# DeltaNet followed by hash routing on one core: 64-column products, another order of the products, and another start and end of the first phase

## The chip, the cores and the metric

One core of a Trainium2 chip. The metric is device microseconds (us) of one execution of the whole kernel; all data are float32. Engines are named as in the profile: PE is TensorE, PEld its weight loads, DVE VectorE, ACT ScalarE, POOL GpSimd, SP the queue from which most DMAs are issued.

## The reference

```python
# q, k, v: (4, 8, 768, 48), beta: (4, 8, 768); token_ids: 3072; w1: (8, 384, 1024); w2: (8, 1024, 384)
k_n = k / (norm(k) + 1e-6)
state = 0                                   # (4, 8, 48, 48)
for t in range(768):
    y[t] = q[t] @ state
    v_old = state.T @ k_n[t]
    state += beta[t] * outer(k_n[t], v[t] - v_old)
x = y as (3072, 384)                        # token = batch and position, columns = head and element
expert = token_ids * 2654435761 % 8
out[token] = relu(x[token] @ w1[expert]) @ w2[expert]
```

## The kernel before, in words

Phase 1 computes `y`. The 768 steps are cut into `NU` = 24 chunks of `C` = 32 steps. Inside a chunk the recurrence becomes a triangular system, so that a chunk is a handful of matrix products; only the 48x48 states go from chunk to chunk. The 32 pairs of batch and head are packed four to a tile of 128 partitions (four blocks of 32), which gives `NT` = 8 tiles, in two halves `h` of `HT` = 4. The state of two heads lies in 96 partitions.

The products of one half of one chunk, each with what comes after it:

- `ks`: old state times K into `psK`. It is written as two products of 64 columns for each tile (`pair(p)`); VectorE then makes `R = V - psK` (L487).
- `ys`: state times Q into `psY`, one product of 128 columns for each tile with 96 moving columns (L494).
- `w`: the inverted triangular matrix `TB` times `R` into `psW`, 128 columns, 48 moving (L500); ScalarE copies it to `W` in two instructions (L504).
- `s`: `K4` times `W`, added to the state in `psS` (L510); ScalarE copies it to `S` (L516).
- `ym`: the masked Gram matrix `MB` times `W`, added to `psY`, 128 columns, 96 moving (L520); of the 96 columns that result, half are used in either half of the partitions. ScalarE copies `psY` to `x_sb` in two instructions (L527), and `store_x` sends it to memory.

Every float32 product appears in the profile as two matmul instructions.

A set is what four chunks of one batch need: `turn_heads` transposes K and Q of a set on TensorE (L347) and spreads them (`sd`, `KT`, `QT`) with ScalarE and, for the first four sets, VectorE; `gram` multiplies them (L382); `gram_out` copies the products to `NT` (ScalarE) and, masked, to `MT` (VectorE, L394). Four sets make a group, enough for four chunks. `invert(g)` inverts a group's triangular matrices on VectorE alone: a chain of some 80 dependent instructions with 31 steps of two tensor_tensor each (L436, L438), at its end the transposition `TU` (L441). It is a generator with an estimate in us ahead of each piece, and `inv.do(us)` issues pieces up to that sum. `spread` copies a chunk's part of `MT` and `TU` into the block-diagonal tiles `MB` and `TB` by four DMAs each, from the SP queue.

The order is written out by hand in one loop over `c` from -9 to 23: every engine runs its instructions in the order of that loop. Iteration `c` computes chunk `c`, turns set `c+9`, multiplies set `c+8`, inverts a quarter of group `c//4+1`, and loads two chunks ahead (`load_k4` and `load_v` from the POOL queue, `load_kq` from SP). From the iteration after 16 on, `routing` (one-hot ranks of the tokens, mostly VectorE, with three groups of matmuls) is advanced two to four pieces at the end of each iteration; its two products `rp` (L221, L222) and the four groups `gp` (L317) wait for VectorE. Weights of the first expert are loaded at the end of iteration 16.

Before the loop, 16 DMAs of `beta` are issued from ScalarE's queue (L160), POOL builds constants and clears 11 tiles (L180), and VectorE makes the mask `low` (L175).

Phase 2 gathers the tokens of each expert and runs the two products (L636, L650). The change does not touch it.

The loop of one iteration before:

```python
ks(c, 0); inv.do(2.4); ys(c, 0); w(c, 0); ks(c, 1); s(c, 0); s_out(c, 0); ym(c, 0); y_out(c, 0); w(c, 1)
inv.do(5.6); scale_v(c + 1); store_x(c - 1); turn_k(ut); tq = turn_q(ut)
ys(c, 1); s(c, 1); s_out(c, 1); next(tq); gram(ug, 0); ym(c, 1); y_out(c, 1)
gram(ug, 1); gram_out(ug); spread(MT, MB); spread(TU, TB)
```

Of the kernel before, what the change touches and what calls it, by code (L numbers as in the profile page):

```python
# [18 lines left out]
def kernel(  # L19
# [12 lines left out]
    P = 128  # L32
# [52 lines left out]
    with ExitStack() as phase1:  # L85
# [22 lines left out]
        def quarter(q):  # L108
            return slice(C * q, C * q + C)
# [42 lines left out]
        load_kq(0)  # L152
        load_kq(1)

        beta_i = st.tile([P, NG, C], F32)
        beta_r = beta.rearrange("b (g q) (n c i) -> q c (b g) n i", q=4, c=GC, i=C)
        for i in range(4):
            for j in range(GC):
                p0 = C * i + NT * j
                nc.scalar.dma_start(out=beta_i[p0:p0 + NT], in_=beta_r[i, j])  # L160
# [18 lines left out]
        for t in W2s + TBs + MBs + K4s:  # L179
            nc.gpsimd.memset(t, 0.0)  # L180


        def routing():
# [34 lines left out]
            yield  # L218
# [3 lines left out]
            nc.tensor.matmul(rp[:, 1], lhsT=ones, rhs=oh, start=True, stop=True)  # L222
            rank = rt.tile([P, E, NTC], F32)
# [4 lines left out]
            yield  # L228
# [5 lines left out]
            yield  # L234
# [14 lines left out]
            yield  # L249
# [9 lines left out]
            yield  # L259
# [14 lines left out]
                                    op=ALU.mult)  # L274
            yield
            col = rt.tile([P, E, NTC], F32)
            for i in range(1, KT + 1):
# [11 lines left out]
            yield  # L289
# [16 lines left out]
                                    op=ALU.mult)  # L306
            yield
            val = rt.tile([P, NHI], F32)
            G = 6
            for g in range(NTC // G):  # L310
                lo = rt.tile([P, G, P], F32, name="lo")
                nc.vector.tensor_tensor(
                    lo, iota_f[:, None, :].to_broadcast([P, G, P]),
                    part[:, 1, g * G:(g + 1) * G, None].to_broadcast([P, G, P]), op=ALU.is_equal)
                gp = ps_t.tile([P, NHI], F32, tag="t")
                for i in range(G):
                    nc.tensor.matmul(gp, lhsT=lo[:, i], rhs=hi[:, g * G + i],  # L317
                                     start=(i == 0), stop=(i == G - 1))
                if g == 0:
                    nc.vector.tensor_copy(val, gp)  # L320
                else:
                    nc.vector.tensor_tensor(val, gp, val, op=ALU.add)
                yield
# [14 lines left out]
            yield  # L338
# [4 lines left out]
        def turn_heads(u, x, dst, a):  # L343
            g, b = divmod(u, B)
            psT = ps_t.tile([D2, H // 2, GC, C], F32, tag="t", name="psT")
            for i in range(H // 2):
                nc.tensor.transpose(psT[:, i].rearrange("p j s -> p (j s)"),  # L347
                                    x[:, 2 * i:2 * i + 2].rearrange("p h d -> p (h d)"), ident)

            sd = sds[u][:, :, a].rearrange("p j i s -> p i j s")  # L350
# [5 lines left out]
            yield  # L356
# [7 lines left out]
        def turn_k(u):  # L364
            sds[u] = pre.tile([D2, GC, 2, H // 2, C], F32, tag="sd", bufs=2, name="sd")
            for _ in turn_heads(u, Kd.pop(u), KTs, 0):
                pass

        def turn_q(u):
            return turn_heads(u, Qd.pop(u), QTs, 1)  # L370
# [15 lines left out]
        def gram_out(u):  # L386
# [3 lines left out]
            psG = psGs.pop(u)  # L390
            del sds[u]
            nc.scalar.activation(NTs[g][:, :, :, 2 * b:2 * b + 2].rearrange("p t j g -> p g j t"),
                                 psG[:, :, :, 0], ACT.Copy)
# [66 lines left out]
        def spread(src, dst):  # L460

            for i in range(4):
                nc.sync.dma_start(out=dst[quarter(i), :, i, :], in_=src[quarter(i)])
# [25 lines left out]
        def ys(c, h):  # L489
            Ys[h] = ps_y.tile([P, HT, 2, D], F32, tag="y", name="psY")  # L490
            if c == 0:
                return
            for i, QT in enumerate(tiles(QTs, c, h)):
                nc.tensor.matmul(Ys[h][:, i], lhsT=QT.rearrange("p u x -> p (u x)"),  # L494
                                 rhs=Ss[h][:, i], start=(i == 0), stop=True, skip_group_check=True)

        def w(c, h):
            psW = ps_w.tile([P, HT, D], F32, tag="w", name="psW")
            for i in range(HT):
                nc.tensor.matmul(psW[:, i], lhsT=TBs[c % 2][:, HT * h + i], rhs=Rs[h][:, i],  # L500
                                 start=True, stop=True, skip_group_check=True)
# [16 lines left out]
        def ym(c, h):  # L518
            for i in range(HT):
                nc.tensor.matmul(Ys[h][:, i], lhsT=MBs[c % 2][:, HT * h + i], rhs=Ws[h][:, i],  # L520
                                 start=(c == 0 and i == 0), stop=True, skip_group_check=True)

        def y_out(c, h):
            if h == 0:
                xs[c] = wk.tile([P, NT, D], F32, tag="x_sb", bufs=2, name="x_sb")
            for p in range(2):
                nc.scalar.activation(xs[c][pair(p), HT * h:HT * h + HT], Ys[h][pair(p), :, p],  # L527
                                     ACT.Copy)
# [8 lines left out]
        route = None  # L537
        inv = Work(iter(()))
        for c in range(-9, NU):
            step = c >= 0  # L540
            ut, ug = c + 9, c + 8
            turns, grams = ut < NU, 0 <= ug < NU
            if c % GC == 0 and c // GC + 1 < NG and c >= -GC:
                inv = Work(invert(c // GC + 1))
            if ut + 2 < NU:
                load_kq(ut + 2)
            if c >= -4 and c + 2 < NU and c + 2 >= 0:
                load_k4(c + 2)
                load_v(c + 2)
            if step:  # L550
                ks(c, 0)
            inv.do(2.4 if step else 3.0)
            if step:
                ys(c, 0)
                w(c, 0)
                ks(c, 1)
                s(c, 0)
# [5 lines left out]
            if c + 1 >= 0 and c + 1 < NU:  # L563
                scale_v(c + 1)
            if c >= 1:
                store_x(c - 1)
            if turns:
                turn_k(ut)
                tq = turn_q(ut)
            else:  # L570
                tq = iter(())
            if step:
                ys(c, 1)
                s(c, 1)
                s_out(c, 1)
            next(tq, None)
            if grams:
                gram(ug, 0)
# [3 lines left out]
            for _ in tq:  # L582
                pass
            if grams:
                gram(ug, 1)
                gram_out(ug)
            if -1 <= c < NU - 1:
                n = c + 1
                spread(MTs[n // GC % 3][:, n % GC], MBs[n % 2])
                spread(TUs[n // GC][:, n % GC], TBs[n % 2])  # L590
            if route is not None:
# [172 lines left out]
```

## Time and profile before

| what | us |
|---|---|
| time, median of 3 runs (lowest to highest) | 746.71 (745.66 to 749.37) |
| the profiled execution, its own time | 746.85 |
| its span | 745.2 |
| PE busy (share of the span) | 645.9 (87%) |
| DVE busy | 286.6 (38%) |
| ACT busy | 206.0 (28%) |
| POOL busy | 190.7 (26%) |
| chunk 0 begins (first `w`) | 65.17 |
| chunk 15 begins | 281.95 |
| phase 1's last `ym` begins | 406.10 |
| phase 2's first gemm begins | 426.64 |

The profile is of one execution. Its page gives busy shares of each engine over the whole span; since phase 1 and phase 2 have different limits, the same shares are asked for by stretches, and then the instructions of one chunk in order of time. The rows merge neighbouring instructions of one kind and one line into one row with a count, and a square bracket says how long the engine sat idle just before and who released it. PEclk is the clock that TensorE was granted, as a share of 2.4 GHz: 0.5 is 1.2 GHz.

### The profile page before, as it was taken

What the parts mean: (1) busy time and instruction counts of PE and PEld (TensorE: products, weight loads), DVE (VectorE), ACT (ScalarE), POOL (GpSimd) and SP (SyncE); (2) the same over time, 40 slices, a digit from 0 to 9 for tenths busy, and PEclk for the clock granted to TensorE, in tenths of its full rate; (3) what the DMA queues carried; (4) which work ended last, traced back from release to release, by engine and by line L of the source; (5) the groups of instructions that cost most, each with busy time, mean ns of one, the idle gap of its engine ahead of it and who ended that gap; (6) DMA issues with size and microseconds to landing.
All of it is one profiled execution on the core that took longest, in us unless ns stands there. A gap on an engine that the chain in (4) does not pass through costs nothing. (4 is left out here: it accounts for less than half of the span.)

```text
span 745.2 us, 11251 instructions
## 1 busy us (share of the span) xinstructions
PE 645.9 (87%) x4212; PEld 474.3 (64%) x4212; DVE 286.6 (38%) x725; ACT 206.0 (28%) x461; POOL 190.7 (26%) x293
## 2 busy tenths in 40 slices
PE   4545989998998999958988399999999999999995
PEld 3435888888888888857878155555555555555552
DVE  7697564574762584756421211111212110212110
ACT  2633454564545454312302010101011111101010
POOL 9200432243233225323400601040404040202022
PEclk9955787798878689868957599999999999999998
DMA  7622444354444333832410893242424220101011
GB/s 143 129 39 48 94 86 85 70 106 93 85 89 83 58 57 72 224 62 53 88 26 18 263 352 112 84 145 84 149 84 152 84 65 0 31 0 32 0 35 30
DMA packets 151112, 65.39 MB, mean 88 GB/s; under 512 B 134089, under 2 KB 143155, under 8 KB 151057
## 3 DMA queue, kind: packets, MB, share of 16 engines
q1 hardware_dynamic: 139920, 45.66, 25.5%
q0 software_dynamic: 10240, 18.89, 10.3%
q8 instruction: 35, 0.57, 0.3%
q10 hardware_dynamic: 896, 0.10, 0.1%
q14 instruction: 21, 0.16, 0.1%
HBM read 49.67 MB, written 10.22 MB: 80 GB/s over the span
## 5 line engine op out<-in xcount | busy, mean ns | idle before, releaser
L636 PE MATMUL h_ps<-xT,w_sb 128*128 128x448 f32 x384 | 147.4, 544 | 0.0
L650 PE MATMUL y_ps<-h_sb,w_sb 128*128 128x448 f32 x384 | 146.1, 539 | 0.0
L636 PEld LDWEIGHTS h_ps<-xT,w_sb 128*128 128x128 f32 x384 | 73.7, 192 | 72.1 <-issue 71.9
L650 PEld LDWEIGHTS y_ps<-h_sb,w_sb 128*128 128x128 f32 x384 | 72.2, 190 | 67.6 <-issue 67.6
L144 POOL DMA_DIRECT2D K<-in_k_dram x96 | 55.6, 586 | 194.8 <-PE psS L510 193.5
L641 DVE TENSOR_SCALAR h_sb<-h_ps 128x448 f32<-128x448 f32 x32 | 20.0, 625 | 168.3 <-PE h_ps L636 168.3
L619 POOL DMA_INDIRECT xg<-x_scratch,gx x32 | 31.9, 997 | 189.0 <-PE xT_ps L628 138.0
L500 PE MATMUL psW<-R,TB 128*128 128x48 f32 x368 | 58.8, 312 | 20.0 <-DVE R L487 20.0
L500 PEld LDWEIGHTS psW<-R,TB 128*128 128x128 f32 x368 | 56.3, 233 | 23.0 <-DVE R L487 22.8
L520 PE MATMUL psY<-W,MB 128*128 128x96 f32 x384 | 70.4, 344 | 0.2 <-ACT W L504 0.2
L520 PEld LDWEIGHTS psY<-W,MB 128*128 128x128 f32 x384 | 65.3, 256 | 1.5 <-ACT W L504 0.3
L438 DVE TENSOR_TENSOR U<-U,tmp 128x31 f32<-128x31 f32 (+15 forms) x186 | 63.7, 342 | 6.4
L436 DVE TENSOR_TENSOR tmp<-U,Ni 128x31 f32<-128x31 f32 (+15 forms) x186 | 63.5, 342 | 5.6
L510 PE MATMUL psS<-W,K 128*96 128x96 f32 x368 | 56.5, 317 | 6.9 <-ACT W L504 5.5
L664 POOL DMA_INDIRECT out_dram<-o_sb,gidx x32 | 30.5, 953 | 120.9 <-ACT o_sb L662 111.0
L494 PE MATMUL psY<-S,QT 96*128 96x96 f32 x368 | 59.1, 312 | 0.8 <-ACT x_sb L527 0.8
L510 PEld LDWEIGHTS psS<-W,K 128*96 128x96 f32 x368 | 49.5, 222 | 9.9 <-ACT W L504 7.7
L150 POOL DMA_DIRECT2D V<-in_v_dram x96 | 55.3, 583 | 1.8 <-issue 1.7
L494 PEld LDWEIGHTS psY<-S,QT 96*128 96x128 f32 x368 | 53.1, 222 | 2.9 <-ACT x_sb L527 1.4
L504 ACT ACTIVATE W<-psW 64x192 f32<-64x192 f32 x96 | 31.1, 324 | 81.5 <-PE psW L500 79.7
L639 ACT ACTIVATE h_sb<-h_ps 128x448 f32<-128x448 f32 x32 | 17.4, 543 | 130.3 <-PE h_ps L636 107.3
L382 PE MATMUL psG<-sd,KT 96*64 96x64 f32 x768 | 36.2, 250 | 18.5 <-DVE MT L394 18.5
(126 smaller groups left out, 570.5 us busy)
## 6 DMA issues: line engine op xcount, KB each, us to landing
w_sb<-in_moe_w_dram SPq DMA_DIRECT2D x16, 1536.0 KB
Kd<-in_k_dram SPq DMA_DIRECT2D x24, 192.0 KB
Qd<-in_q_dram SPq DMA_DIRECT2D x24, 192.0 KB
K<-in_k_dram POOLq DMA_DIRECT2D x96, 48.0 KB, 2.9
V<-in_v_dram POOLq DMA_DIRECT2D x96, 48.0 KB, 2.5
x_scratch<-x_sb SPq DMA_DIRECT2D x96, 48.0 KB
MB<-MT SPq DMA_DIRECT2D x96, 32.0 KB
TB<-TU SPq DMA_DIRECT2D x96, 32.0 KB
```

The lines of the kernel that those rows point to most:

```text
L144: nc.gpsimd.dma_start(out=K4s[c % 3][quarter(i), :, i % 2, :], in_=k_r[i, c * C:(c + 1) * C])
L150: nc.gpsimd.dma_start(out=Vs[c][quarter(i)], in_=v_r[i, c * C:(c + 1) * C])
L382: nc.tensor.matmul(psG[pair(p), hg, j], lhsT=KT[:, j, hg, p].rearrange("p r s -> p (r s)"), rhs=sd[:, j, :, 2 * hg + p], start=True, stop= ...
L436: V.tensor_tensor(tmp, U[:, 0:n, j:j + 1].to_broadcast([P, n, m]), Ni[:, j:j + 1, j + 1:].to_broadcast([P, n, m]), op=ALU.mult)
L438: V.tensor_tensor(U[:, 0:n, j + 1:], U[:, 0:n, j + 1:], tmp, op=ALU.add)
L494: nc.tensor.matmul(Ys[h][:, i], lhsT=QT.rearrange("p u x -> p (u x)"), rhs=Ss[h][:, i], start=(i == 0), stop=True, skip_group_check=True)
L500: nc.tensor.matmul(psW[:, i], lhsT=TBs[c % 2][:, HT * h + i], rhs=Rs[h][:, i], start=True, stop=True, skip_group_check=True)
L510: nc.tensor.matmul(psS[h][:, i], lhsT=K4s[c % 3][:, HT * h + i], rhs=Ws[h][:, i], start=(c == 0 and i == 0), stop=True, skip_group_check=True)
L520: nc.tensor.matmul(Ys[h][:, i], lhsT=MBs[c % 2][:, HT * h + i], rhs=Ws[h][:, i], start=(c == 0 and i == 0), stop=True, skip_group_check=True)
L619: nc.gpsimd.indirect_dma_start(out=xg[0:TS], out_offset=None, in_=x_dram[:, :], in_offset=bass.IndirectOffsetOnAxis(ap=idx[0:TS], axis=0), ...
L636: nc.tensor.matmul(h_ps[:, :width], lhsT=w1_sb[:, co, fo * P:(fo + 1) * P], rhs=xT[:, co, :width], start=(co == 0), stop=(co == CO - 1))
L650: nc.tensor.matmul(y_ps[:, :width], lhsT=w2_sb[:, fo, co * P:(co + 1) * P], rhs=h_sb[:, fo, :width], start=(fo == 0), stop=(fo == FO - 1))
```

## The change

All products of 128 columns in a chunk are split in two of 64 (`ys`, `w`, `ym`), as `ks` was; `psY` then holds only the used columns, and `y_out` is one instruction. The order of the products changes: K's transpositions go between `ys` and `w` of the first half, Q's between `ks` of the second half and `s` of the first. The mask of the Gram products (`mt_out`) moves from the end of an iteration to the next one, behind `ks` of the second half. `MB` is spread from the POOL queue at the start of the iteration before it is used. The first group's four sets are prepared in a loop of their own; three sets instead of two are loaded at the top; `beta` is loaded from the POOL queue after the constants, ahead of the clearing of the tiles. Routing starts two iterations later and is cut so that VectorE's pieces come in the middle of an iteration and TensorE's at the end; the one-hot products `gp` go into one bank as 64-column halves.

```diff
-        load_kq(0)
-        load_kq(1)
-        beta_i = ...
-                nc.scalar.dma_start(out=beta_i[p0:p0 + NT], in_=beta_r[i, j])
+        for u in range(3):
+            load_kq(u)
...
-        for t in W2s + TBs + MBs + K4s:
+        beta_i = ...
+                nc.gpsimd.dma_start(out=beta_i[p0:p0 + NT], in_=beta_r[i, j])
+        for t in K4s + W2s + TBs + MBs:
             nc.gpsimd.memset(t, 0.0)
...
             for r in range(2):
+                yield
-                if u < B and (a == 0 or r == 0):
+                if u < B and r == 0:
                     nc.vector.tensor_scalar(out=to[:, :, :, r], in0=psT, ...)
                 else:
                     nc.scalar.activation(to[:, :, :, r], psT, ACT.Copy, scale=own[:, r:r + 1])
...
         def ys(c, h):
-            Ys[h] = ps_y.tile([P, HT, 2, D], F32, tag="y", name="psY")
+            Ys[h] = ps_y.tile([P, HT, D], F32, tag="y", name="psY")
             for i, QT in enumerate(tiles(QTs, c, h)):
-                nc.tensor.matmul(Ys[h][:, i], lhsT=QT.rearrange("p u x -> p (u x)"),
-                                 rhs=Ss[h][:, i], ...)
+                for p in range(2):
+                    nc.tensor.matmul(Ys[h][pair(p), i], lhsT=QT[:, p], rhs=Ss[h][:, i, p], ...)
         def w(c, h):
-                nc.tensor.matmul(psW[:, i], lhsT=TBs[c % 2][:, HT * h + i], rhs=Rs[h][:, i], ...)
+                for p in range(2):
+                    nc.tensor.matmul(psW[pair(p), i],
+                        lhsT=TBs[c % 2][:, HT * h + i, 2 * p:2 * p + 2].rearrange("k r t -> k (r t)"),
+                        rhs=Rs[h][:, i], ...)
         def ym(c, h):
-                nc.tensor.matmul(Ys[h][:, i], lhsT=MBs[c % 2][:, HT * h + i], rhs=Ws[h][:, i], ...)
+                for p in range(2):
+                    nc.tensor.matmul(Ys[h][pair(p), i],
+                        lhsT=MBs[c % 2][:, HT * h + i, 2 * p:2 * p + 2].rearrange("k r t -> k (r t)"),
+                        rhs=Ws[h][:, i, p], ...)
         def y_out(c, h):
-            for p in range(2):
-                nc.scalar.activation(xs[c][pair(p), HT * h:HT * h + HT], Ys[h][pair(p), :, p], ACT.Copy)
+            nc.scalar.activation(xs[c][:, HT * h:HT * h + HT], Ys[h], ACT.Copy)
...
+        for u in range(B):
+            tk, tq = turn_heads(u, 0), turn_heads(u, 1)
+            for it in (tk, tq, tk, tq, tk, tk, tq, tq):
+                next(it, None)
+            if u + 3 < B + 2:
+                load_kq(u + 3)
+            if u > 0:
+                gram(u - 1, 0); gram(u - 1, 1); nt_out(u - 1); mt_out(u - 1)
+        gram(B - 1, 0); gram(B - 1, 1); nt_out(B - 1); mt_out(B - 1)
-        for c in range(-9, NU):
+        for c in range(-5, NU):
...
+            if 1 <= c:
+                store_x(c - 1)
...
+                spread(MTs[n // GC % 3][:, n % GC], MBs[n % 2], nc.gpsimd)
             ks(c, 0)
-            inv.do(2.4 if step else 3.0)
+            inv.do(2.0 if step else 3.0)
             ys(c, 0)
+            upto(tk, 3)
             w(c, 0)
+            upto(tk, 1)
             ks(c, 1)
+            upto(tq, 1)
             s(c, 0); s_out(c, 0); ym(c, 0); y_out(c, 0)
+            mt_out(waiting)
-            inv.do(None if c % GC == GC - 1 else 5.6)
+            inv.do(None if c % GC == GC - 1 else 6.0)
+            for part in route:
+                if part == "PE":
+                    break
             scale_v(c + 1)
+            w(c, 1)
+            upto(tq, 2)
             ys(c, 1)
+            gram(ug, 0)
             s(c, 1); s_out(c, 1)
+            gram(ug, 1)
+            upto(tq, 1)
             ym(c, 1); y_out(c, 1)
+            nt_out(ug); waiting = ug
-            spread(MTs[n // GC % 3][:, n % GC], MBs[n % 2])
-            spread(TUs[n // GC][:, n % GC], TBs[n % 2])
+            spread(TUs[n // GC][:, n % GC], TBs[n % 2], nc.sync)
-            for _ in range(2 if c < NU - 3 else 4):
-                next(route, None)
+            next(route, None)
...
+            if c == NU - GC - 2:
                 route = routing()
```

## Rows read from the trace of the kernel before

**Rows 1.** Busy time (count) by stretch: start:end, length, PE, PEld, DVE, ACT, POOL, PEclk, DMA share, GB/s
```profile
65.17:281.95 216.78, 196.16 (x1992) 184.22 (x1994) 127.71 (x360) 111.18 (x256) 69.51 (x119) 0.80 0.43 82
281.95:407.16 125.21, 106.66 (x938) 101.11 (x934) 58.40 (x167) 33.21 (x92) 34.67 (x62) 0.77 0.38 79
426.76:745.20 318.44, 310.62 (x946) 164.19 (x945) 45.04 (x84) 33.58 (x64) 52.33 (x54) 0.99 0.26 86
384.00:399.00 15.00, 15.00 (x97) 14.63 (x97) 3.16 (x14) 2.92 (x8) 0.00 (x0) 0.50 0.00 0
```

**Rows 2.** TensorE in order of time, chunk 8: start us, us, engine line op xcount
```profile
179.31 0.62 PE L484 MATMUL psK<-S,KT 96*64 96x48 f32 x16
179.86 1.13 PE L494 MATMUL psY<-S,QT 96*128 96x96 f32 x8
182.13 1.09 PE L500 MATMUL psW<-R,TB 128*128 128x48 f32 x8 [1.13 <-DVE R L487]
...
184.33 1.59 PE L510 MATMUL psS<-W,K 128*96 128x96 f32 x8 [0.51 <-ACT W L504]
185.72 1.92 PE L520 MATMUL psY<-W,MB 128*128 128x96 f32 x8
...
188.43 0.60 PE L347 MATMUL psT<-ident,Kd 128*96 128x128 f32 x4
...
189.74 0.84 PE L510 MATMUL psS<-W,K 128*96 128x96 f32 x8
...
190.94 0.69 PE L382 MATMUL psG<-sd,KT 96*64 96x64 f32 x16
```

**Rows 3.** TensorE in order of time, first product of chunk 22
```profile
384.44 1.10 PE L484 MATMUL psK<-S,KT 96*64 96x48 f32 x16
```

**Rows 4.** VectorE in order of time: first and last instruction in chunks 8, 1, 2
```profile
181.39 0.42 DVE L394 TENSOR_TENSOR MT<-psG,low 128x256 f32<-128x256 f32 x1 [10.04 <-ACT NT L392]
...
190.24 0.55 DVE L456 TENSOR_TENSOR V<-V,NV 128x384 f32<-128x384 f32 x1
...
78.71 0.42 DVE L394 TENSOR_TENSOR MT<-psG,low 128x256 f32<-128x256 f32 x1 [5.87 <-ACT NT L392]
...
89.55 0.55 DVE L456 TENSOR_TENSOR V<-V,NV 128x384 f32<-128x384 f32 x1
...
95.44 0.42 DVE L394 TENSOR_TENSOR MT<-psG,low 128x256 f32<-128x256 f32 x1 [5.34 <-ACT NT L392]
...
106.42 0.56 DVE L456 TENSOR_TENSOR V<-V,NV 128x384 f32<-128x384 f32 x1
...
111.24 2.06 DVE L441 STREAM_TRANSPOSE TU<-U 128x1024 f32<-128x1024 f32 x1
```

**Rows 5.** In order of time, the start of the kernel and chunk 0's first product
```profile
2.12 8.04 DVE L175 TENSOR_SCALAR low_i<-low_i 128x32 int32<-128x32 int32 x1 [2.12 <-POOL low_i L173]
...
4.25 1.06 PE L347 MATMUL psT<-ident,Kd 128*96 128x128 f32 x4 [4.25 <-DMA Kd<-in_k_dram]
...
10.38 0.68 DVE L352 COPY sd<-psT 96x512 f32<-96x512 f32 x1
...
30.17 1.24 DVE L404 STREAM_TRANSPOSE Ni<-NT 128x1024 f32<-128x1024 f32 x1
...
65.17 1.92 PE L500 MATMUL psW<-V,TB 128*128 128x48 f32 x8 [1.78 <-DMA TB<-TU]
```

**Rows 6.** TensorE in order of time, routing's first product and its last group
```profile
324.39 0.98 PE L221 MATMUL rp<-onehot,ups 128*128 128x192 f32 x2 [7.68 <-DVE onehot L215]
...
381.71 2.80 PE L317 MATMUL gp<-hi,lo 128*128 128x53 f32 x12 [1.17 <-DVE lo L312]
```

**Rows 7.** POOL and VectorE in order of time, two places where both work
```profile
149.82 2.30 POOL L144 DMA_DIRECT2D K<-in_k_dram  x4 [8.39 <-PE psS L510]
...
150.24 0.42 DVE L438 TENSOR_TENSOR U<-U,tmp 128x256 f32<-128x256 f32 x1
...
297.55 0.97 DVE L412 TENSOR_SCALAR sq<-Ni 128x32 f32<-128x32 f32 x1
```

More of the change, by code (lines that the diff above doesn't have):

```diff
@@ L178 @@
         nc.vector.tensor_tensor(low, low_i[:, 0], low_i[:, 1], op=ALU.is_lt)
-        for t in W2s + TBs + MBs + K4s:
+        beta_i = st.tile([P, NG, C], F32)
+        beta_r = beta.rearrange("b (g q) (n c i) -> q c (b g) n i", q=4, c=GC, i=C)
+        for i in range(4):
+            for j in range(GC):
+                p0 = C * i + NT * j
+                nc.gpsimd.dma_start(out=beta_i[p0:p0 + NT], in_=beta_r[i, j])
+        for t in K4s + W2s + TBs + MBs:
             nc.gpsimd.memset(t, 0.0)
@@ L306, in routing @@
                                     op=ALU.mult)
+            yield "PE"
+            yield
+            lo = [rt.tile([P, NTC // 4, P], F32, name=f"lo{g}") for g in range(4)]
+            for g in range(4):
+                G = NTC // 4
+                nc.vector.tensor_tensor(
+                    lo[g], iota_f[:, None, :].to_broadcast([P, G, P]),
+                    part[:, 1, g * G:(g + 1) * G, None].to_broadcast([P, G, P]), op=ALU.is_equal)
+            yield "PE"
+            gp = ps_t.tile([P, NHI], F32, tag="t")
+            for i in range(NTC):
+                for p in range(2):
+                    nc.tensor.matmul(gp[pair(p)], lhsT=lo[i * 4 // NTC][:, i % (NTC // 4), pair(p)],
+                                     rhs=hi[:, i], start=(i == 0), stop=(i == NTC - 1),
+                                     skip_group_check=True)
             yield
             val = rt.tile([P, NHI], F32)
[L309 to L323, printed above, removed]
+            nc.vector.tensor_copy(val, gp)
             none = rt.tile([P, NHI], F32)
@@ L493, in ys @@
             for i, QT in enumerate(tiles(QTs, c, h)):
-                nc.tensor.matmul(Ys[h][:, i], lhsT=QT.rearrange("p u x -> p (u x)"),
-                                 rhs=Ss[h][:, i], start=(i == 0), stop=True, skip_group_check=True)
+                for p in range(2):
+                    nc.tensor.matmul(Ys[h][pair(p), i], lhsT=QT[:, p], rhs=Ss[h][:, i, p],
+                                     start=(i == 0), stop=True, skip_group_check=True)
         def w(c, h):
@@ L499, in w @@
             for i in range(HT):
-                nc.tensor.matmul(psW[:, i], lhsT=TBs[c % 2][:, HT * h + i], rhs=Rs[h][:, i],
-                                 start=True, stop=True, skip_group_check=True)
+                for p in range(2):
+                    nc.tensor.matmul(
+                        psW[pair(p), i],
+                        lhsT=TBs[c % 2][:, HT * h + i, 2 * p:2 * p + 2].rearrange("k r t -> k (r t)"),
+                        rhs=Rs[h][:, i], start=True, stop=True, skip_group_check=True)
             Ws[h] = W2s[(2 * c + h) % 4]
@@ L519, in ym @@
             for i in range(HT):
-                nc.tensor.matmul(Ys[h][:, i], lhsT=MBs[c % 2][:, HT * h + i], rhs=Ws[h][:, i],
-                                 start=(c == 0 and i == 0), stop=True, skip_group_check=True)
+                for p in range(2):
+                    nc.tensor.matmul(
+                        Ys[h][pair(p), i],
+                        lhsT=MBs[c % 2][:, HT * h + i, 2 * p:2 * p + 2].rearrange("k r t -> k (r t)"),
+                        rhs=Ws[h][:, i, p], start=(c == 0 and i == 0), stop=True,
+                        skip_group_check=True)
         def y_out(c, h):
@@ L533, in store_x, with upto @@
             del xs[c]
-        route = None
+        def upto(it, n):
+            for _ in range(n):
+                next(it, None)
+        for u in range(B):
+            tk, tq = turn_heads(u, 0), turn_heads(u, 1)
+            for it in (tk, tq, tk, tq, tk, tk, tq, tq):
+                next(it, None)
+            if u + 3 < B + 2:
+                load_kq(u + 3)
+            if u > 0:
+                gram(u - 1, 0)
+                gram(u - 1, 1)
+                nt_out(u - 1)
+                mt_out(u - 1)
+        gram(B - 1, 0)
+        gram(B - 1, 1)
+        nt_out(B - 1)
+        mt_out(B - 1)
+        route, waiting = iter(()), None
         inv = Work(iter(()))
-        for c in range(-9, NU):
+        for c in range(-5, NU):
             step = c >= 0
             ut, ug = c + 9, c + 8
-            turns, grams = ut < NU, 0 <= ug < NU
-            if c % GC == 0 and c // GC + 1 < NG and c >= -GC:
+            tk = tq = iter(())
+            if c % GC == 0 and c // GC + 1 < NG:
                 inv = Work(invert(c // GC + 1))
+            if 1 <= c:
+                store_x(c - 1)
             if ut + 2 < NU:
                 load_kq(ut + 2)
-            if c >= -4 and c + 2 < NU and c + 2 >= 0:
+            if c >= -4 and 0 <= c + 2 < NU:
                 load_k4(c + 2)
                 load_v(c + 2)
+            if -1 <= c < NU - 1:
+                n = c + 1
+                spread(MTs[n // GC % 3][:, n % GC], MBs[n % 2], nc.gpsimd)
             if step:
                 ks(c, 0)
-            inv.do(2.4 if step else 3.0)
+            inv.do(2.0 if step else 3.0)
             if step:
                 ys(c, 0)
+            if ut < NU:
+                tk = turn_heads(ut, 0)
+                upto(tk, 3)
+            if step:
                 w(c, 0)
+            upto(tk, 1)
+            if step:
                 ks(c, 1)
+            if ut < NU:
+                tq = turn_heads(ut, 1)
+                upto(tq, 1)
+            if step:
                 s(c, 0)
@@ L560 @@
                 y_out(c, 0)
-                w(c, 1)
-            inv.do(None if c % GC == GC - 1 else 5.6)
[L563 to L571, printed above, removed]
+            if waiting is not None:
+                mt_out(waiting)
+                waiting = None
+            inv.do(None if c % GC == GC - 1 else 6.0)
+            for part in route:
+                if part == "PE":
+                    break
+            if 0 <= c + 1 < NU:
+                scale_v(c + 1)
+            if step:
+                w(c, 1)
+            upto(tq, 2)
             if step:
                 ys(c, 1)
+            if B <= ug < NU:
+                gram(ug, 0)
+            if step:
                 s(c, 1)
                 s_out(c, 1)
-            next(tq, None)
-            if grams:
-                gram(ug, 0)
+            if B <= ug < NU:
+                gram(ug, 1)
+            upto(tq, 1)
             if step:
```

54 lines of the change are left out of this document (20 added, 34 removed).

## The prediction, made before the changed kernel ran

> **What bounds the kernel now.** I read the busy time by stretch first, then TensorE's instructions of one chunk in order of time, then VectorE's, then the start and routing. The stretches [rows 1] show three limits. From 426.76 us to the end TensorE is busy 310.6 of 318.4 us at clock 0.99; the change leaves these instructions alone, and I carry that part over unaltered, with the 19.6 us of gathering ahead of it (407.16 to 426.76). The gain has to come from the first 407.2 us. There TensorE is busy 196 of 217 us in chunks 0 to 14 (14.45 us each), but at a granted clock of 0.80, a mix of 2.4 and 1.2 GHz; VectorE is busy 59% of it and ScalarE 51%.
>
> One chunk [rows 2] shows how the two engines hold each other. After the first `ks` and `ys`, TensorE sits 1.13 us until VectorE has made `R`, and later 0.51 us until ScalarE has made `W`. Behind these gaps the clock drops: `s` takes 1.59 us there and 0.84 us five us later. VectorE, in turn, stood idle 10.04 us in that round and 5 to 6 us in others [rows 4], not for lack of work (an inversion was waiting) but because the mask `MT` is first in its queue and needs the Gram product from the very end of the iteration; `R` stands behind it. So TensorE's amount of work bounds a chunk, and the place of `MT` adds gaps to it.
>
> **The split products.** `ks` is the row to price them by: it already runs as 64-column pairs, sixteen instructions in 0.62 us, the next group starting 0.55 us after it. `ys` takes 1.13 us and `w` 1.09 us for the same four tiles [rows 2]; `ym` has the moving columns of `ys`, and I put it at 1.13. After the change all three have sixteen instructions of 64 columns with 48 moving, as `ks`. They contract over 128 rows where `ks` has 96; the bounds are 0.62 (as `ks`) and the present 1.1 (the pair gains nothing), and I take 0.62, the row of the same shape. At full clock a chunk's durations are then 2 x (4 x 0.62 + 0.84 for `s` + 0.60 for a transposition group + 0.69 for a Gram group) = 9.2 us; fourteen groups overlap their followers by 0.07 us each, which leaves 8.2 us. The same sum for before is 11.2 us plus 1.6 us of gaps; the rest up to 14.45 is the low clock.
>
> Here a rule speaks against the change. The Trainium skill, TensorEngine Tiling, section Instruction Overhead, says that each matmul has some 60 cycles of overhead, that fewer moving columns than that save nothing, and that a tiling factor should not be taken from a dimension that is already small. By that, twice as many instructions of 48 columns would save nothing, and the sum would be that of rival B. The trace's `ks` does not agree: 39 ns for each of its instructions against 136 ns for each of `w` with the same 48 columns.
>
> **The order.** K's transpositions now stand between `ys` and `w`, Q's between `ks` and `s`: 0.60 us of work each in front of the two places that waited. `MT` goes behind the second `R`, so that the inversion no longer waits for it. What is late next is VectorE itself. Its work from first to last instruction is 9.4 us in the first chunk of a group, 11.4 and 11.5 in the next two [rows 4], and in the fourth some 3.8 (`TU` 2.06, `MT` 0.42, two `R` of its kind, `V` 0.55). The new budgets (2.0 and 6.0 for 2.4 and 5.6) have the same sum; by the estimates in the code one step of the inversion moves from the second chunk to the first, one from the third to the second: 10.1, 11.6, 10.6, 3.8. In three of four chunks that is more than TensorE's 8.2, so TensorE will wait, in one gap ahead of the first `w`.
>
> **The POOL queue.** It gets four more DMAs per chunk. Four issues take 2.30 us [rows 7], so twelve take 6.9. VectorE's tensor_tensor beside them keeps its 0.42 us, so I charge VectorE nothing. But the clearing of `U` for each inversion stands behind all twelve: 7.9 us after the queue starts, where VectorE comes to its first write of `U` about 6 us into the chunk (in chunk 8 it came 4.7 us after `MT`). I charge 1.4 us to the first chunk of a group; bounds 0 (the queue starts before the chunk does) and 3. `MB` itself is needed a whole iteration later. SP loses the four issues.
>
> **Chunks 0 to 14.** First chunk of a group 11.5, second 11.6, third 10.6, fourth TensorE's 8.2 and 0.7 for what the low clock leaves over; with 0.2 each for handing over, 43.4 a group. Three groups and three more chunks: 164 us, where it is 216.8: 53 us less. The clock is in this: after a VectorE gap of 2 to 3 us I expect some 6 us at 1.2 GHz, as behind the gap of 1.13 us. That is some 6 us of slow products and 4.6 us of fast ones, still within VectorE's 11.
>
> **The start.** VectorE's first instruction takes 8.04 us for 32 columns, until POOL has cleared its tiles, and the first copy of a transposed K is at 10.38, though K was transposed at 5.3 [rows 5]. In the new order 16 DMA issues stand between the two, as long as that instruction now lasts, so the copy starts near 5.5: 4.9 us. Of VectorE's four operations for each of the first four sets one, of about 0.7 us, goes to ScalarE: 4 x 0.7 = 2.8 us. Together 8 us (30.17 becomes 22 for the first inversion; what follows up to 65.17 stays 35 us long). Bounds: 1, if the clearing, now beside the sets' copies, holds those copies as it held the first instruction (it held a tensor_scalar of an SBUF tile to 0.97 us at 297.55 [rows 7]; no row shows one that reads PSUM), and 10.
>
> **Chunks 15 to 23.** Now 125.2 us at clock 0.77. TensorE waited 7.68 us for the one-hot ranks and took 12.5 us for the four `gp` groups with their waits (the last group 2.80 us at low clock) [rows 6]; chunk 22 behind them ran 15 us at 0.50. After: chunk 15 8.5; 16 to 18 VectorE's 11.5, 11.6, 10.6, plus 2 for transfers behind the expert's weights; 19 10.8 (its one-hot ranks wait for POOL's constants, which now stand behind twelve DMAs); 20 9; 21 9.5; 22 12.5 with all `gp` products (96 instructions of 39 ns, 3.7 us); 23 6.5. Sum 92.5, so 33 us less. Bounds 20 (low clock throughout) and 43.
>
> **Sum.** 8 + 53 + 33 = 94 us. The profiled execution took 746.85 us, 1.65 beside its span, and stands at the median of 746.71: 746.85 - 94 gives 653 us.
>
> **Rivals.**
> A, the forecast: 653 us (its own range 640 to 670).
> B, the 64-column halves gain nothing with 128 rows: a chunk's products then take 8.2 + 6 x 0.48 = 11.1 us, with the low clock of before 13.2; 15 of them 198 (19 less), the tail 21 less, the start 8: 699 us. For it: no row has 64 columns with 128 rows. Against it: `ks` and the Gram pairs.
> C, the slower side: the clock falls in the VectorE gap and does not come back within the chunk. At 1.2 GHz `ks` takes 1.10 [rows 3] and `s` 1.59; with transpositions and Gram products at 1.8 times their rows a chunk's durations are 2 x (4.40 + 1.59 + 1.08 + 1.24) = 16.6, less overlap, plus waits 16.4: 246 us, 29 more than before; the tail 13 less, the start 8 less: 755 us. It decides from a chunk of 14.45 + (8 + 13)/15 = 15.9 us on, that is, a granted clock under about 0.52 from chunk 0 to 14. For it: from 384 to 399 TensorE was busy all the 15 us and stayed at 0.50. Against it: in chunk 8 the clock came back within six us, and a TensorE without gaps, as this would be, did so in most chunks.
> D, the clock recovers late: 12.5 us a chunk (29 less), tail 27 less, start 6 less: 685 us.
> E, VectorE alone sets the pace, with no wait for `U`, 10.3 a chunk (62 less), tail 43, start 10: 632 us.
>
> The Trainium skill (TensorE: Matmul & The Clock Gate, Part 1) says that the half rate is the default and activity releases it. Chunk 22 agrees only in part: TensorE had no gap there, and the half rate stayed.
>
> **Chances.** A 0.50, E 0.20, D 0.15, B 0.10, C 0.05. The predicted time is A's. With E's and D's edges, B within, and room for a tail worse than I put it, the range is 626 to 699. A measurement of this kernel tells 0.5% (3.7 us) from no change. All but C are faster by more; between C and B little probability lies near 747: faster 0.93, within 0.5% 0.02, slower 0.05.
>
> **What would show it.** Right: `w`, `ys`, `ym` at some 0.62 us for sixteen instructions at full clock; chunk times repeating 11.5, 11.6, 10.6, 9; the first `w` of a chunk released by VectorE after 2 to 3 us, with `MT` no longer waiting for ScalarE; the first inversion near 22 us, chunk 0 near 57; phase 2's first gemm near 332. Wrong: a `w` near 1.1 us (B); a granted clock near 0.5 through the chunks (C, D); VectorE's instructions longer beside POOL's DMAs; the first copy still near 10 us. If chunks all last alike and VectorE idles, not VectorE but TensorE or ScalarE is the bound, and the size of the gain is wrong even if its sign is right.

## The result and the profile after

The changed kernel takes 650.72 us (median; 647.53 to 653.40), beside 746.23 us for the kernel before: a ratio of 0.871, 95% interval [0.866, 0.876]. The forecast was 653 us. Ratios here and below leave out executions over 1.5% above the fastest of their kernel; medians are over all. The profiled execution took 650.86 us with a span of 649.3 us; the profiled one of before took 96.0 us more, 95.9 us of them in the span.

First the busy time by stretch, with columns as in [rows 1]: chunks 0 to 14, chunks 15 to 23, the gathering, and the rest.
```profile
57.90:216.50 158.60, 133.26 (x2692) 119.21 (x2694) 127.87 (x349) 104.99 (x229) 100.28 (x173) 0.91 0.66 111
216.50:305.33 88.83, 71.41 (x1418) 64.51 (x1414) 61.12 (x176) 26.80 (x74) 54.84 (x96) 0.83 0.54 113
305.33:325.33 20.00, 3.82 (x16) 2.44 (x16) 5.05 (x12) 0.33 (x1) 10.05 (x10) 0.56 0.72 221
325.33:649.30 323.97, 310.48 (x947) 164.11 (x945) 45.07 (x84) 33.61 (x64) 52.41 (x54) 0.98 0.25 85
```
Against [rows 1], the start is 7.3 us shorter (65.17 to 57.90), chunks 0 to 14 58.2 us, chunks 15 to 23 36.4 us; the gathering is 0.4 us longer and the last stretch 5.5 us. That sums to 95.9. TensorE is now busy 84% of chunks 0 to 14 (133.26 of 158.60) where it was 90%, and VectorE 81% where it was 59%: the bound has moved to VectorE, in three chunks of four, as the waits below show.

TensorE in order of time, parts of chunks 6 to 9 (the third and fourth of a group, the first and second of the next), to set beside [rows 2]:
```profile
121.17 0.67 PE L493 MATMUL psY<-S,QT 96*64 96x48 f32 x16
121.78 0.64 PE L347 MATMUL psT<-ident,Kd 128*96 128x128 f32 x4
124.34 0.68 PE L500 MATMUL psW<-R,TB 128*64 128x48 f32 x15 [1.93 <-DVE R L485]
...
125.96 0.84 PE L512 MATMUL psS<-W,K 128*96 128x96 f32 x8
126.73 0.67 PE L523 MATMUL psY<-W,MB 128*64 128x48 f32 x16
...
135.08 0.68 PE L500 MATMUL psW<-R,TB 128*64 128x48 f32 x15 [2.43 <-DVE R L485]
...
143.31 0.67 PE L500 MATMUL psW<-R,TB 128*64 128x48 f32 x16
...
154.73 1.16 PE L500 MATMUL psW<-R,TB 128*64 128x48 f32 x16 [1.94 <-DVE R L485]
...
157.56 1.49 PE L512 MATMUL psS<-W,K 128*96 128x96 f32 x8
```
`w`, `ys` and `ym` take 0.67 us for their sixteen instructions at full clock. The wait for `R` stands where it was forecast, and in three chunks of four: the `w` of chunk 8 at 143.31, which ends the fourth chunk of a group, comes without one. From the first `w` of a chunk to the first of the next, chunks 4 to 7 take 11.41, 11.70, 10.74 and 8.23 us.

Now waits from 55 to 220 us: engine, line, what was waited for, us in total, times, longest.
```profile
PE psW L500 <- DVE R L485: 20.2, 10, 2.4
...
DVE R L485 <- PE psK L482: 17.2, 7, 5.5
...
PE psS L512 <- ACT W L506: 4.0, 6, 1.0
DVE U L424 <- POOL U L406: 2.8, 2, 1.4
...
PE psW L500 <- DMA TB<-TU: 1.9, 2, 1.0
```
The waits of `MT` for the Gram product, 5 to 10 us each in [rows 4], are gone from the list. What VectorE still waits for is `ks`, up to 5.5 us, at the end of the fourth chunk of a group: there TensorE is the later one. The forecast wait for `U` is there, in two chunks. VectorE in order of time, in chunks 8, 12 and 16, the first of their groups:
```profile
148.82 0.20 DVE L424 COPY U<-b 128x32 f32<-128x32 f32 x1 [1.41 <-POOL U L406]
...
190.61 1.84 DVE L423 TENSOR_SCALAR nb<-b 128x32 f32<-128x32 f32 x1
...
237.49 0.20 DVE L424 COPY U<-b 128x32 f32<-128x32 f32 x1 [3.29 <-POOL U L406]
```
Chunk 4 has the 1.41 us of chunk 8. In chunk 12 there is no wait, but the instruction ahead, 0.42 us in chunk 8, takes 1.84 and ends with POOL's clearing of `U` (191.44 to 192.41); chunks 8 and 12 both take 11.42 us.

Last the start, VectorE and POOL in order of time:
```profile
2.12 0.18 DVE L168 TENSOR_SCALAR low_i<-low_i 128x32 int32<-128x32 int32 x1 [2.12 <-POOL low_i L166]
...
5.14 0.69 DVE L355 COPY sd<-psT 96x512 f32<-96x512 f32 x1 [2.54 <-PE psT L347]
...
13.22 0.74 DVE L362 TENSOR_SCALAR KT<-psT,own 96x512 f32<-96x512 f32 x1
...
22.12 1.24 DVE L402 STREAM_TRANSPOSE Ni<-NT 128x1024 f32<-128x1024 f32 x1
```
```profile
2.13 6.85 POOL L178 DMA_DIRECT2D beta_i<-in_beta_dram  x12
...
11.58 2.11 POOL L180 MEMSET K<- 128x768 f32 x3
13.62 1.52 POOL L180 MEMSET W<- 128x384 f32 x4
```
The instruction that took 8.04 us in [rows 5] takes 0.18, the first copy comes at 5.14, and the first inversion at 22.12 (forecast: 22). POOL clears from 11.58 on beside VectorE's work on the sets, and the tensor_scalar at 13.22 keeps its 0.74 us.

### The profile page after: what moved, and what is told of

Same layout as the page of the kernel before. It is cut to its first block, busy times and chain, and to the rows that moved or that the text cites. A ratio compares the mean times of both kernels' runs of the same rounds, so it can differ in the third digit from the quotient of the medians.

```text
span 649.3 us, 13500 instructions
## 1 busy us (share of the span) xinstructions
PE 547.9 (84%) x5396; PEld 372.9 (57%) x5396; DVE 278.3 (43%) x718; ACT 195.3 (30%) x417; POOL 255.2 (39%) x405
## 4 chain that ended last, share of the span: by engine, by line
PE 39%; issue 9%; DMA 1%; POOL 1%; DVE 1%; SPq 0%; POOLq 0%; DVEq 0%
PE h_ps L675 20%; PE y_ps L689 17%; PE xT_ps L667 1%; PE o_ps L698 1%; DMA xg<-x_scratch,gx 1%; POOL out_dram L703 1%; DVE xg L735 0%; SPq L536 0%; DMA x_scratch<-x_sb 0%; POOLq L798 0%; DVE o_sb L701 0%; DVE xT L669 0%; DVEq L712 0%; POOLq L703 0%; POOL xg L658 0%
## 5 line engine op out<-in xcount | busy, mean ns | idle before, releaser
L500 PE MATMUL psW<-R,TB 128*64 128x48 f32 x736 | 35.9, 242 | 33.5 <-DVE R L485 33.5
L461 POOL DMA_DIRECT2D MB<-MT x96 | 55.5, 585 | 2.6 <-issue 1.3
L512 PE MATMUL psS<-W,K 128*96 128x96 f32 x368 | 49.1, 286 | 8.0 <-ACT W L506 7.7
L500 PEld LDWEIGHTS psW<-R,TB 128*64 128x64 f32 x736 | 30.9, 156 | 37.9 <-DVE R L485 36.8
L691 ACT COPY yT<-y_ps 128x448 f32<-128x448 f32 x16 | 8.5, 532 | 142.0 <-PE y_ps L689 142.0
L377 PE MATMUL psG<-sd,KT 96*64 96x64 f32 x768 | 33.8, 240 | 20.3 <-DVE MT L392 20.3
L512 PEld LDWEIGHTS psS<-W,K 128*96 128x96 f32 x368 | 42.3, 193 | 12.5 <-ACT W L506 11.1
L691 DVE COPY yT<-y_ps 128x448 f32<-128x448 f32 x8 | 5.0, 626 | 90.4 <-PE y_ps L689 90.4
L377 PEld LDWEIGHTS psG<-sd,KT 96*64 96x64 f32 x768 | 28.8, 152 | 24.4 <-DVE MT L392 22.2
```

Of the source, the lines that this page charges most:

```text
L377: nc.tensor.matmul(psG[pair(p), hg, j], lhsT=KT[:, j, hg, p].rearrange("p r s -> p (r s)"), rhs=sd[:, j, :, 2 * hg + p], start=True, stop= ...
L461: eng.dma_start(out=dst[quarter(i), :, i, :], in_=src[quarter(i)])
L500: nc.tensor.matmul(psW[pair(p), i], lhsT=TBs[c % 2][:, HT * h + i, 2 * p:2 * p + 2].rearrange("k r t -> k (r t)"), rhs=Rs[h][:, i], start= ...
L512: nc.tensor.matmul(psS[h][:, i], lhsT=K4s[c % 3][:, HT * h + i], rhs=Ws[h][:, i], start=(c == 0 and i == 0), stop=True, skip_group_check=True)
```

## The experiments

**The split undone, all else kept (e1_no_split).**
```diff
-                for p in range(2):
-                    nc.tensor.matmul(
-                        psW[pair(p), i],
-                        lhsT=TBs[c % 2][:, HT * h + i, 2 * p:2 * p + 2].rearrange("k r t -> k (r t)"),
-                        rhs=Rs[h][:, i], start=True, stop=True, skip_group_check=True)
+                nc.tensor.matmul(psW[:, i], lhsT=TBs[c % 2][:, HT * h + i], rhs=Rs[h][:, i],
+                                 start=True, stop=True, skip_group_check=True)
...
```


> The changed kernel with its ys, w and ym again as single products of 128 columns (and y_out in two instructions); order, start, queues and routing as changed. Theory 1 (the split takes work from TensorE and the order takes the gaps out, and both are needed before VectorE sets the pace): TensorE needs some 11 to 11.5 us of products per chunk at full clock and more with stretches at 1.2 GHz, so chunks come to 12.5 to 13 us and TensorE no longer waits 2 us for R; about 690 us. Rival 1 (the order alone brings VectorE to the pace, the split is hidden behind VectorE): 655 to 660 us. Rival 2 (the order brings nothing, only start and routing): about 712 us.

Measured: 672.86 us, ratio 0.900 [0.893, 0.907]. The size was a miss: I had left the clock low. The stretch 65 to 215 us of this kernel:
```profile
65.00:215.00 150.00, 145.96 (x1806) 134.47 (x1805) 112.04 (x307) 102.85 (x231) 92.75 (x159) 1.00 0.64 107
```
With the long products and the new order TensorE is busy 97% at a granted clock of 1.00, in chunks of 11.07 to 11.66 us, and its waits for `R` sum to 0.2 us there. So the new order, with `MB` on POOL's queue, takes away both the gaps and the low clock without the split; TensorE's 11.1 us and VectorE's work then nearly match.

**The split alone, in the order of before (e2_split_only).** The same edit to `ys`, `w`, `ym` and `y_out` the other way round, made to the kernel before.

> The kernel before with nothing but the split: ys, w, ym as pairs of 64 columns, y_out in one instruction; order, start, queues and routing as before. Theory 1: the mask MT still stands ahead of R and waits for the last Gram product, so the gap ahead of w grows from 1.1 to some 1.6 us and a chunk stays near 12.4 us; the routing stalls stay; about 700 us. Rival 1 (the split alone brings everything that the chunks gained): about 665 us with only start and routing missing. Rival 2 (halves with 128 rows gain nothing): 740 us or more, w at 1.1 us at full clock.

Measured: 688.4, 693.2, 701.1 and 703.2 us, beside 748.65 for the kernel before; no interval. The profile is of the execution of 693.2. The times are nearest to theory 1 and exclude rival 2; the gap ahead of `w`, forecast as 1.6 us, is 1.4 on average. Its stretch and its waits from 65 to 215 us:
```profile
65.00:215.00 150.00, 123.09 (x2302) 110.28 (x2302) 106.25 (x300) 85.79 (x195) 58.80 (x101) 0.84 0.58 107
```
```profile
DVE MT L394 <- ACT NT L392: 34.6, 8, 7.6
...
PE psW L502 <- DVE R L487: 19.6, 14, 2.5
```
VectorE still stands idle for the Gram product and TensorE's gaps stay, with the clock at 0.84. Split alone is worth some 58 us by the two shortest executions (52 by the median of four), all the rest alone 76, and both 96: they remove in part the same loss, and then VectorE's work is the floor. On top of the other edits the split brings 22 us (672.86 to 650.72): in the profiled executions 2.3 in the start, 6.3 from chunk 1 to 14, nearly 12 from chunk 15 to 23.

**MB by SyncE's queue (e3_mb_sp).** This and the next run ask what the new bound still costs.
```diff
-                spread(MTs[n // GC % 3][:, n % GC], MBs[n % 2], nc.gpsimd)
+                spread(MTs[n // GC % 3][:, n % GC], MBs[n % 2], nc.sync)
```


> The changed kernel with MB's four DMAs issued from SP instead of POOL, at the same place in the program. Theory 1 (POOL's twelve issues hold back the clearing of U in the first chunk of each group): VectorE's wait for U, 1.4 us in a chunk and 3.3 in one, goes, 5 to 8 us in all. Theory 2 (POOL's last drain, which now ends 7.8 us behind the last scatter and ended 2.1 us behind it before, gets longer with the number of DMAs that POOL issued): the end after the last scatter goes from 8.6 back to some 3 to 4 us. Both: 638 to 642 us. Neither: 650. Rival (SP becomes the bound, MB comes late in the chunks while the expert's weights are loaded): 655 or more.

Measured: 654.9 us, ratio 0.876 [0.870, 0.881], which overlaps the changed kernel's. In the trace both theories came true: VectorE no longer waits for `U`, and from the last scatter to the end of the span it is 3.6 us for 8.6. But the last `ym` begins at 314.53 for 304.41, since SyncE took more in the chunks:
```profile
PE psW L500 <- DMA TB<-TU: 15.2, 12, 2.8
PE psW L500 <- DVE R L485: 11.2, 7, 3.4
```
`TB`, next in that queue, makes TensorE wait 12 times. The rival held in that SyncE's queue became a bound; it named `MB` and the time of the expert's weights, where it was `TB`, and before them.

**Budget 4.6 for 6.0 (e4_even).**
```diff
-            inv.do(None if c % GC == GC - 1 else 6.0)
+            inv.do(None if c % GC == GC - 1 else 4.6)
```


> The changed kernel with the second inversion budget at 4.6 instead of 6.0, so that a fourth of the inversion moves from the first three chunks of a group to the fourth. Theory 1 (VectorE sets the pace in three of four chunks, TensorE in the fourth): the first three lose some 1.7 us each, the fourth gains 1.5 to 2; some 3 us a group, 636 to 640 us. Rival (TensorE with its clock sets the pace and VectorE's gap only fills time): 650 us, or more if the late TU holds back the next group's first w.

Measured: 650.64 us, ratio 0.870 [0.865, 0.875]. VectorE's work was evened out, and the wait moved. The fourth chunk, in order of time:
```profile
136.32 2.15 DVE L439 STREAM_TRANSPOSE TU<-U 128x1024 f32<-128x1024 f32 x1 [0.56 <-DMA Qd<-in_q_dram]
138.53 2.59 SPq L461 DMA_DIRECT2D TB<-TU  x4
...
142.00 0.42 PE L500 MATMUL psW<-R,TB 128*64 128x48 f32 x2 [3.33 <-DMA TB<-TU]
```
The steps taken from the first three chunks stand ahead of `TU`, whose transfer the next `w` needs. Chunks 5 to 7 take 9.7, 9.3 and 11.6 us for 11.7, 10.7 and 8.2: the same sum. The rival held.

**Beta ahead of the constants again (e5_start).**
```diff
+                nc.scalar.dma_start(out=beta_i[p0:p0 + NT], in_=beta_r[i, j])
...
-                nc.gpsimd.dma_start(out=beta_i[p0:p0 + NT], in_=beta_r[i, j])
```


> The changed kernel with one step put back: beta is loaded by ScalarE's queue ahead of the constants, so POOL's clearing of the tiles stands right behind the constants, as it did before the change, and not behind beta's 16 DMA issues. Theory: the clearing then holds VectorE's first instructions again; the first of them ends near 8 us instead of 2.3, the first copy of a transposed K comes near 10 us, the first inversion 5 us later than 22.1, and the whole takes 655 to 657 us. Rival: the four sets are paced by their transfers and by TensorE, the copies have slack, and the first inversion stays within 1 us of 22.1; the time is that of the changed kernel, 650 us.

Measured: 657.96 us, ratio 0.884 [0.877, 0.892]: 7.2 us above the changed kernel. Its VectorE in order of time:
```profile
2.12 8.04 DVE L174 TENSOR_SCALAR low_i<-low_i 128x32 int32<-128x32 int32 x1 [2.12 <-POOL low_i L172]
...
10.39 0.68 DVE L355 COPY sd<-psT 96x512 f32<-96x512 f32 x1
...
27.95 1.24 DVE L402 STREAM_TRANSPOSE Ni<-NT 128x1024 f32<-128x1024 f32 x1
```
The 8.04 us are back to the digit, and the first inversion is 5.8 us later. So of the 8.05 us by which it came earlier (30.17 to 22.12), the place of the clearing is worth 5.8. The other 2.2 are gained in this run too; they fit the operation that went to ScalarE, put at 2.8, but the third set loaded at the top and the loop of its own were not tried apart from it.

**U cleared ahead of the loads (e6_u_first).**
```diff
+            U = wk.tile([P, C, C], F32, tag="U", bufs=1, name="U")
+            nc.gpsimd.memset(U, 0.0)
             yield 1.3
...
-            U = wk.tile([P, C, C], F32, tag="U", bufs=1, name="U")
-            nc.gpsimd.memset(U, 0.0)
```


> The changed kernel with one step moved: the clearing of U stands ahead of the chunk's DMA issues in POOL's queue and not behind them. Theory: VectorE's waits for U in the first chunk of each group (1.4 us each, 3.3 in chunk 16) are part of the pace, because VectorE is the bound there; they go, each such chunk is 1.4 us shorter, and the whole takes some 8 us less, 641 to 644 us. Rival: the wait only moves (to the transfers of TB, as in the run with the even budget), 648 to 651 us.

Measured: 646.47 us (644.60 to 649.08), ratio 0.869 [0.863, 0.875]; the interval overlaps the changed kernel's. In the trace the wait for `U` is gone, the first chunks of a group take 9.7 to 10.4 us for 11.4 (chunk 16 10.0 for 13.4), the clock of 65 to 215 us is 0.95 for 0.93, and the last `ym` begins at 298.45 for 304.41. From the first `w` to there it is 7.3 us less, near the 8 expected; the start was 1.35 us longer. The price of 1.4 us is confirmed by the trace. The median is 4 us lower, the lowest seen, but not clear of the noise.

**MT back in front of R (e8_mt_end).**
```diff
-            if waiting is not None:
-                mt_out(waiting)
-                waiting = None
...
-                waiting = ug
+                mt_out(ug)
```


> The changed kernel with one step put back: the masking into MT stands at the end of the iteration, ahead of the next chunk's first R in VectorE's queue. Theory: VectorE again waits there for ScalarE's reading of the Gram tile, so R comes later and TensorE's gap ahead of w grows by 1 to 3 us in every chunk that still has a Gram product; 16 such chunks make 670 to 690 us. Rival: the new order has the Gram product early enough, the wait is short, and the time stays at 650 to 654 us.

Measured: 650.62 us, ratio 0.873 [0.866, 0.881]: the rival held. Its VectorE in order of time:
```profile
123.47 0.42 DVE L392 TENSOR_TENSOR MT<-psG,low 128x256 f32<-128x256 f32 x1
123.80 0.35 DVE L485 TENSOR_TENSOR R<-V,psK 128x192 f32<-128x192 f32 x1
...
142.30 0.42 DVE L392 TENSOR_TENSOR MT<-psG,low 128x256 f32<-128x256 f32 x1 [4.89 <-ACT NT L386]
```
In the chunks that VectorE paces it comes to `MT` after the Gram tile is ready; where it waits (142.30), `R` would have waited for `ks` anyway, 3.98 us in the changed kernel.

**The routing of before (e9_routing).**
```diff
+                    nc.tensor.matmul(gp, lhsT=lo[:, i], rhs=hi[:, g * G + i],
+                                     start=(i == 0), stop=(i == G - 1))
...
-            if c == NU - GC - 2:
+            if c == NU - 2 * GC:
```


> The changed kernel with the routing of before: its steps, their stepping at the end of each iteration, the begin three chunks earlier, and four gp groups of full 128-column products with a wait between each. Theory: TensorE again waits for the one-hot ranks and for the gp groups, and the clock falls behind them; chunks 15 to 23 get 15 to 25 us longer, 665 to 675 us. Rival: the gain of chunks 15 to 23 came from the split products and the order, and routing alone is worth under 5 us: 650 to 655 us.

Measured: 668.90 us, ratio 0.898 [0.889, 0.907]: 18 us above the changed kernel. (Routing begins two iterations earlier here, not three as expected above.) TensorE in order of time, this kernel and then the changed one:
```profile
254.70 0.98 PE L220 MATMUL rp<-onehot,ups 128*128 128x192 f32 x2 [4.84 <-DVE onehot L214]
...
308.38 2.80 PE L316 MATMUL gp<-hi,lo 128*128 128x53 f32 x12 [1.17 <-DVE lo L311]
```
```profile
272.41 0.59 PE L220 MATMUL rp<-onehot,ups 128*128 128x192 f32 x2
...
297.31 2.98 PE L315 MATMUL gp<-hi,lo 128*64 128x53 f32 x96
```
The chunk with the four groups takes 24.8 us, and the last `ym` begins 19.4 us later. Routing is about half of the 36 us that chunks 15 to 23 gained.

**Three ways to a better version.** MB by ScalarE's queue, with U cleared first:

> The changed kernel with U cleared ahead of the DMA issues, and MB spread by ScalarE's queue in place of POOL's. Theory 1: POOL then issues 276 DMAs and not 368, its end behind the last scatter falls from 7.8 to about 2.8 us, and ScalarE, busy two thirds of the chunks, has room for four issues of 0.4 us each: 5 us less than with U alone, some 641 us. Theory 2: the issues of 1.6 us delay ScalarE's W and S, which TensorE waits for; 24 chunks get 0.5 to 1 us longer each and the end's gain is lost: 648 to 665 us.

Measured: 655.92 us, ratio 0.881 [0.870, 0.892]. ScalarE in order of time shows theory 2:
```profile
123.26 1.97 ACTq L461 DMA_DIRECT2D MB<-MT  x3
125.33 0.59 ACT L357 ACTIVATE sd<-psT 96x512 f32<-96x512 f32 x1 [1.93 <-DMA MB<-MT]
```
Three issues take 1.97 us there, ScalarE's next copy waits 1.93 us for the last of them, and TensorE's waits for `W` sum to 15.0 us between 55 and 220 us, where they were 2.2 with U alone. (POOL issues 272 DMAs here; the expectation's 276 was a miscount.)

The rest of the inversion at the first place of the fourth chunk, budgets 2.4 and 5.0:

> The changed kernel with U cleared ahead of the DMA issues, with inversion budgets of 2.4 and 5.0 for 2.0 and 6.0, and with all that is left of the inversion done at the first place of the fourth chunk and not half at its second, so that TU is there in time for its transfer. Theory: VectorE's work is what sets the pace of three chunks of a group, while it idles over 5 us in the fourth; with this the group takes about 39 us in place of 40.7, and the kernel 639 to 642 us. Rival: R of the fourth chunk, now behind 4.7 us of the inversion, makes TensorE wait there as long as it gains before: 646 to 650 us.

Measured: 649.59 us, ratio 0.876 [0.866, 0.886]. A group takes 39.9 us (9.40, 9.62, 10.58, 10.30) for 41.1 with U alone, but the fourth chunk grows, as the rival had it (8.2 to 8.6 with U alone). The stretch 215 to 305 us then ran at clock 0.73 for 0.88 of the run with U first, and the gain is lost there. Why the clock is lower there is open.

Both together, and both with budgets 2.0 and 4.6:

> Both of these: budgets of 2.4 and 5.0 with the rest at the first place of the fourth chunk, and MB by ScalarE's queue. If the two gains are of separate places they add: 634 to 638 us. If ScalarE is the next bound, 645 us or more.

> As the run before it with budgets of 2.0 and 4.6: first three chunks shorter, 6.8 us of the inversion ahead of the second R of the fourth. Theory: the sum of a group is VectorE's work of some 36 us plus handing over, and falls by another 0.6 us to 38.3: 632 to 637 us. Rival: the fourth chunk grows by more than the others lose, since R is then 2 us late there: 640 us or more.

Measured: 660.09 us, ratio 0.886 [0.877, 0.895], and 668.87 us, ratio 0.900 [0.892, 0.908]. So the gains don't add. TensorE waits 17.7 and 20.4 us for `W` between 55 and 220 us, as with `MB` by ScalarE's queue alone. In the second the clock of 65 to 215 us is also lower, 0.83 for 0.90; how much of its 9 us that is, was not tried.

## Why the prediction was right, step by step

**The split products** came out as priced by `ks`: 0.67 us for sixteen, estimate 0.62, and not the 1.1 of rival B. That is 42 ns for an instruction of 64 columns, where one of 128 took 136 [rows 2]. The Trainium skill (TensorEngine Tiling, Instruction Overhead) gives each matmul an overhead of some 60 cycles and advises against taking a tiling factor from a dimension that is already small. At 2.4 GHz 60 cycles are 25 ns (an estimate from the page's figure), less than either row; so rival B, which the prediction drew from it, does not follow from that overhead, and the trace does not agree with B.

**The order** did what was said in sum, for a reason half right. TensorE's gaps did shrink to one ahead of `w`, and VectorE did become the bound in three chunks of four. But taking `MT` from the head of its queue was not what did it: put back, it costs nothing (650.62 us). The Gram product now comes early enough, since VectorE is the later one; which of the moved pieces ended the wait was not tried apart.

**VectorE's pace**, 11.5, 11.6, 10.6 and 8.9, each plus 0.2, was measured from chunk 4 on as 11.4, 11.7, 10.7 and 8.2 to 9.8. The stretch of chunks 0 to 14 is 158.6 us for the forecast 164. Measured from first `w` to first `w` it is 162.9; the rest is the place where the stretch ends, as the `w` of chunk 15 comes 4.3 us after its `ks` (220.81 after 216.50).

**The wait for U** was put at 1.4 us in the first chunk of each group. It is 1.41 in chunks 4 and 8, the same delay within a longer instruction in chunk 12, and 3.29 in chunk 16; chunk 0 has none. Taken away, it gave some 4 us in the median: the mechanism of rival E, but 646 us and not 632.

**The clock** came out better than in rivals C and D: 0.91 in chunks 0 to 14. After some gaps it fell for about six us, as behind the 1.94 us at 154.73, where `s` took 1.49 us; after others, as the 1.93 us at 124.34 or the 2.43 at 135.08, it did not fall at all. That it cost little, as forecast, shows in chunks 5, 9 and 13: each takes 11.70 us, with some 3, 6 and 4 us at the low clock.

**The start** was put at 8 us and is 7.3. Of the two terms the clearing was put at 4.9 us and is worth 5.8 in the run with beta ahead of the constants; for the 2.8 the same run leaves 2.2.

**Chunks 15 to 23** were put at 92.5 us and took 88.8. The chunk with the `gp` products was priced 12.5 us and took 9.6: they take 2.98 us in one run, without a wait. The ranks, charged to chunk 19, came without a wait too (9.2 us for 10.8). The 2 us for transfers behind the expert's weights are shown by no run: in the changed kernel TensorE waits for no `TB` there, and what makes chunk 16 take 13.4 us is the 3.29 us for `U`.

**The end** was carried over unaltered and is 5.5 us longer. This step failed, though the surplus of the other terms hides it in the sum. The work is the same (TensorE busy 310.48 for 310.62 us); what grew is what follows the last scatter (below). That 653 is so near to 650.72 is in part luck: chunks 0 to 14 gained 5 us more than forecast and chunks 15 to 23 3 us more, the start 0.7 less, and the last two stretches lost 5.9 that were put at nothing.

## What to carry to other kernels

Price a split from a row of the same shape in the same trace, and price a new order by the work of the engine that will be second, chunk by chunk: that gave the chunks that VectorE paces to 0.3 us. When two edits remove the same gaps, their gains don't add; here 58 and 76 made 96. Look what stands behind a DMA that is moved to another queue: here `U` waited on POOL, `TB` on SyncE and `W` on ScalarE, and on POOL the end of the program grew as well.

## What the runs showed of the hardware

The end of the program grew with the DMAs that POOL issued, by about 0.05 us for each. The last scatter of the changed kernel, and of the kernel with MB by SyncE's queue:
```profile
639.75 0.95 POOL L703 DMA_INDIRECT out_dram<-o_sb,gidx  x1 [0.30 <-issue]
```
```profile
649.48 0.94 POOL L703 DMA_INDIRECT out_dram<-o_sb,gidx  x1 [0.30 <-issue]
```
The spans end at 649.3 and 654.0, so 8.6 and 3.6 us after them. By number of POOL's DMAs: 256 (before, and split alone) 2.95 us, 272 (MB by SyncE's queue, or by ScalarE's) 3.6, 352 (beta by ScalarE's) 8.0, 368 (the changed kernel and six more runs) 8.5 to 8.6. So `MB`'s 96 cost 5.0 us against either other queue, and beta's 16 some 0.6. DMAs of both kinds made 32 packets each, so the runs can't tell the number of DMAs from that of packets.

POOL's clearing held VectorE's tensor_scalar on an SBUF tile for 8.04 us, and another one in chunk 12 for 1.84 us, each ending as the clearing ended; it did not hold the tensor_scalar that reads PSUM (0.74 us beside it). That reading PSUM is what spares it was not tried by itself.

TensorE, busy 97% of 150 us with the long products, was granted 1.00, while in [rows 1] 15 us without any gap stayed at 0.50 from 384 us on. No run here tells why.
